# Second-layer input products by a seven-product block scheme for two of three token groups

## The chip, the core and the metric

The kernel runs on one core of a Trainium2 chip. The metric is the device time of one execution in microseconds (us), lower is better. The engines are named as in the profile: PE (TensorE, matrix products; PEld is its loading of weights), DVE (VectorE), ACT (ScalarE), POOL (GpSimd) and SP (the queue that issues DMAs). PE writes to PSUM, which has eight banks of 128 x 512 float32; DVE and ACT read them.

## What is computed

Attention with a local window and a few global keys over 2 batches, 8 heads and 768 tokens, and then two feed-forward layers on the 1536 x 512 result. The weights are float64 in memory, q, k and v float32.

```python
x = attn_out.transpose(0, 2, 1, 3).reshape(1536, 512)
h = x @ w_in                       # 512 x 2048
x = (h * (1 / (1 + exp(-h)))) @ w_out      # 2048 x 512
h = x @ w2_in
out = np.maximum(0.01 * h, h) @ w2_out
```

## The kernel before

**Numbers.** Every matrix is held as two float32r halves, a high part and a remainder (hi, lo), side by side in one tile `[128, 2, 512]`. A product takes three passes, hi x hi, lo x hi and hi x lo (`PASSES`, L103), so each 128-wide block of the inner dimension is three matmuls of 128 x 512. A remainder is one DVE subtraction after the copy that rounds the high part.

**Tiling.** The 1536 tokens are three groups (gi = 0, 1, 2) of 512. The 2048 inner columns are four parts of four chunks of 128. For each layer L, part and group, a *unit in* (`unit_in`, L286) multiplies the four 128-blocks of x with one chunk of w_in (12 matmuls into a bank `ph`), applies the nonlinearity (ACT L313 or L315, DVE L320 or L322) and splits the result into `g` (ACT L325, DVE L328). A *unit out* (`unit_out`, L339) multiplies the part's four `g` with w_out (12 matmuls into `po`) and adds to the running sum `y` (ACT L372 in the first part, DVE L390 after). After the last part of layer 0 the sum becomes the next x (`xn`, ACT L404, DVE L407); of layer 1 it is stored.

**Weights.** `load` (L240) brings one chunk of float64 into a stage tile `st` (SP), turns it into float32 `f` by bit operations (ACT L260, DVE L263, L266, L269), and splits it into `wi` or `wo` (the high part on ACT or DVE, L221 or L219; the remainder on DVE, L275). There are 3 stage buffers, 2 of `f`, 5 of `wi`, 6 of `wo`.

**Order.** `Sched.run` (L137) is a list scheduler that runs while the program is built: each task has an engine, a planned duration, a priority, dependencies and buffers (`SIZES`, L450, says how many); the order that it finds is written out, and every engine then works through its list in that order. The priorities of PE tasks rise with `pos` in the order in which `build` (L419) calls the units: two units of the next group, the four output units of this one, the other two units of the next group.

**Memory.** Attention's tiles (`ld`, `kT`, `a`, `sm`) lie in pools that stay open to the end; the running sums of group 2 reuse the `kT` tiles.

Of the kernel before, what the change touches and what calls it, by code (L numbers as in the profile page):

```python
# [16 lines left out]
P = 128  # L17
# [9 lines left out]
def kernel(  # L27
# [197 lines left out]
    class Moe:  # L225


        def __init__(self, sc, pools, xt, xdone, ykey):
            self.sc = sc
            self.wp, self.sp, self.cv, self.gp, self.tp, self.yp, self.xp, self.ps = pools  # L230
            self.ykey = ykey
# [5 lines left out]
            self.w, self.y, self.ydone, self.g = {}, {}, {}, {}  # L237
            self.pos = 100.0

        def load(self, which, L, fc, prio):  # L240
# [4 lines left out]
            f = Buf("f", lambda: self.cv.tile([P, DM], F32, tag="f", name="f"))  # L245
            w = Buf(tag, lambda: self.wp.tile([P, 2, DM], F32R, tag=tag, name=tag, bufs={"wi": 5, "wo": 6}[tag]))
# [37 lines left out]
            self.w[which, L, fc] = (w, t)  # L284

        def unit_in(self, n, j, c0=0, w=TG):  # L286
# [9 lines left out]
            if (n, j) not in self.g:  # L296
                self.g[n, j] = (Buf("g", lambda: self.gp.tile([P, 2, TG], F32R, tag="g", name="g")), [])
            g, gt = self.g[n, j]
# [40 lines left out]
        def unit_out(self, n, e, c0=0, w=TG):  # L339
# [26 lines left out]
            if part == 0:  # L366
                key = self.ykey(L, gi, e)
                y = self.y[gi, e] = Buf(key, lambda: self.yp.tile([P, TG], F32, tag=key, name="yp"))
# [7 lines left out]
                self.ydone[gi, e] = add("ACT", 0.55, evac, -1.0, (m,), (po, y))  # L376
                return
            y = self.y[gi, e]
            if not last:
# [14 lines left out]
            a = add("DVE", 0.07 + 0.55 * r, acc, -1.0, (m, self.ydone[gi, e]), (po, y, dst))  # L394
            self.ydone[gi, e] = a
            if not last:
                return
# [21 lines left out]
        def build(self, look, halves, first):  # L419

            for L in range(2):
                for part in range(NPART):
                    for which in ("in", "out"):
                        for j in range(FPP):
                            self.load(which, L, part * FPP + j, first(L, part, which, j))
            N = len(self.groups)

            def I(n, js):
                if n in halves:
                    for c0 in (0, 256):  # L430
                        for j in js:
                            self.unit_in(n, j, c0, 256)
                else:
                    for j in js:
                        self.unit_in(n, j)

            I(0, range(FPP))
            for n in range(N):
                if n + 1 < N:
                    I(n + 1, range(look))  # L440
                    for e in range(4):
                        self.unit_out(n, e)
                    I(n + 1, range(look, FPP))
                else:
                    for e in range(3):
                        self.unit_out(n, e)
                    self.unit_out(n, 3, 0, 256)
                    self.unit_out(n, 3, 256, 256)

    SIZES = {"st": 3, "f": 2, "wi": 5, "wo": 6, "g": 6, "t": 3, "ps": 8, "ld": 2, "qT": 3, "A": 2, "AT": 4, "sm": 4}  # L450
    for gi in range(NGR):
        for e in range(4):
            SIZES[f"x{gi}{e}"] = SIZES[f"y{gi}{e}"] = SIZES[f"k{e}"] = 1


    with ExitStack() as es:
# [7 lines left out]
        ld = pool("ld", 2)  # L464
        kp = pool("kT", 1)
        ap_ = pool("a", 2)
        sm = pool("sm", 4)
        ps = pool("ps", 8, space=PSUM)


        mask = const.tile([P, 256], F32, name="mask")
        mask0 = const.tile([P, P], F32, name="mask0")
# [43 lines left out]
        zero = const.tile([P, TG], mybir.dt.bfloat16, name="zero")  # L516
# [140 lines left out]
        def st_A(u):  # L657
# [45 lines left out]
            xdone[t0 // 2][hp].append((o, o + 256, add("DVE", 0.36, lo, n + 1.5, (h,), (pv, x))))  # L703
# [12 lines left out]
        def first(L, part, which, j):  # L716
            if L == 0 and part == 0:
# [3 lines left out]
        mo = Moe(sc, (wp, sp, cv, gp, tp, kp, xp, ps), xt, xdone,  # L721
                 lambda L, gi, e: f"k{e}" if gi == NGR - 1 else f"y{gi}{e}")
# [6 lines left out]
    with tc.If(general != 0), ExitStack() as es:  # L729
# [97 lines left out]
        for g in range(NGR):  # L827
            for hp in range(NHP):
                xb[g][hp].tile = xt[g][hp]
        mo = Moe(sc, (pool("gw"), pool("gstage", 3), pool("gcv", 2), pool("gg", 6), pool("gt", 3), pool("gyp"), xp, ps),  # L830
                 xb, done, lambda L, gi, e: f"y{gi}{e}")
# [33 lines left out]
```

## Time and profile before

| | |
|---|---|
| median of 3 runs (lowest to highest) | 630.77 us (630.51 to 631.47) |
| the profiled execution | 630.69 us |
| its span in the trace | 628.9 us |
| PE, DVE, ACT busy | 616.7, 432.8, 275.8 us |
| PE instructions (matmuls) | 3191 in the trace |

The span is what the trace covers, and 1.8 us of the execution lie outside it. A record of a matmul ends by a model and overlaps the next, so that the time that one costs is the distance between two starts. A few per cent of PE's records are missing from the trace, so a count in a row can be low. Everything up to about 140 us has attention and the first layer's first part interleaved; from there on PE does only units.

### The profile page before, as it was taken

To read this page: it belongs to the slowest core of one execution; us is meant where nothing else is said; L and a number is where in the kernel's file an instruction comes from. 1 tells how busy PE (TensorE), PEld (TensorE's weight loads), DVE (VectorE), ACT (ScalarE), POOL (GpSimd) and SP (SyncE) were. 2 spreads that over 40 slices of the span, in tenths; PEclk is the share of its full clock that TensorE was granted. 3 is DMA by queue.
4 is the path that set the end of the run, shared out by engine and by line. 5 is a ranking of instruction groups with operands and counts; after the bars stand their busy time and mean duration, and the time that the engine had idled before them with its cause. 6 is when DMAs were issued, how large, how long until landed. Compare 5 with 4: busy or idle time off the path is not lost.

```text
span 628.9 us, 8667 instructions
## 1 busy us (share of the span) xinstructions
PE 616.7 (98%) x3191; PEld 501.1 (80%) x3191; DVE 432.8 (69%) x993; ACT 275.8 (44%) x612; POOL 2.2 (0%) x18
## 2 busy tenths in 40 slices
PE   7999999999999999999999999999999999999996
PEld 4687777778888888888888888888888888888885
DVE  6999889889653967396748881776369745954333
ACT  5898878855541244124434453444233233213210
POOL 1000000000000000000000000000000000000000
PEclk8999999999999999999999999999999999999999
DMA  8976445213230323023302330133004110200112
GB/s 189 234 181 165 114 97 141 58 40 128 68 100 1 101 69 100 1 77 91 101 1 65 103 90 11 55 113 95 6 16 132 57 64 1 68 0 18 50 68 72
DMA packets 72673, 49.40 MB, mean 79 GB/s; under 512 B 50480, under 2 KB 67120, under 8 KB 72624
## 3 DMA queue, kind: packets, MB, share of 16 engines
q1 hardware_dynamic: 72336, 48.77, 28.0%
q8 instruction: 27, 0.44, 0.3%
q14 instruction: 22, 0.18, 0.1%
q10 hardware_dynamic: 288, 0.00, 0.0%
HBM read 45.62 MB, written 3.15 MB: 78 GB/s over the span
## 4 chain that ended last, share of the span: by engine, by line
PE 92%; DVE 6%; DMA 1%; issue 0%; ACTq 0%; DVEq 0%; ACT 0%
PE po L358 42%; PE ph L305 41%; PE s L618 3%; PE pa L670 3%; PE pv L690 3%; DVE A L630 1%; PE pt L576 1%; DVE A L653 1%; DVE f L266 1%; DMA nraw<-in_n_local_dram 1%; DVE f L269 0%; DVE wi L275 0%; DVE x L699 0%; DVE f L263 0%; DVE rs L644 0%
## 5 line engine op out<-in xcount | busy, mean ns | idle before, releaser
L305 PE MATMUL ph<-x,wi 128*128 128x512 f32 (+1 forms) x624 | 146.0, 379 | 1.2 <-DVE x L699 0.4
L358 PE MATMUL po<-g,wo 128*128 128x512 f32 x576 | 139.8, 392 | 0.0
L305 PE MATMUL ph<-xn,wi 128*128 128x512 f32 x576 | 136.9, 389 | 0.0
L358 PE MATMUL po<-wo,g 128*128 128x512 f32 (+1 forms) x588 | 136.4, 385 | 0.0
L305 PEld LDWEIGHTS ph<-x,wi 128*128 128x128 f32 x624 | 110.7, 188 | 24.7 <-issue 2.2
L358 PEld LDWEIGHTS po<-wo,g 128*128 128x128 f32 x588 | 108.9, 188 | 22.0
L305 PEld LDWEIGHTS ph<-xn,wi 128*128 128x128 f32 x576 | 108.1, 188 | 22.4
L358 PEld LDWEIGHTS po<-g,wo 128*128 128x128 f32 x576 | 107.1, 188 | 23.1 <-issue 1.3
L328 DVE TENSOR_TENSOR g<-t,g 128x512 fp32r<-128x512 f32 (+1 forms) x100 | 66.6, 669 | 41.5 <-ACT g L325 40.1
L325 ACT ACTIVATE g<-t 128x512 fp32r<-128x512 f32 (+1 forms) x100 | 61.2, 616 | 66.2 <-DVE t L322 37.8
L315 ACT ACTIVATE t<-ph 128x512 f32<-128x512 f32 x48 | 28.6, 596 | 91.4 <-PE ph L305 90.5
L322 DVE TENSOR_TENSOR t<-t,ph 128x512 f32<-128x512 f32 x48 | 32.9, 686 | 37.6 <-ACT t L315 37.6
L260 ACT ACTIVATE st<-st 128x512 f32<-128x512 f32 x64 | 43.0, 672 | 31.9 <-DMA st<-in_moe_w_out_dram 23.7
L390 DVE SCALAR_TENSOR_TENSOR yp<-po,yp 128x512 f32<-128x512 f32 x48 | 33.1, 689 | 32.2 <-PE po L358 32.2
L313 ACT ACTIVATE t<-ph 128x512 f32<-128x512 f32 (+1 forms) x52 | 29.2, 563 | 53.9 <-PE ph L305 53.2
L637 ACT ACTIVATE A<-A,nm 128x256 f32<-128x256 f32 (+1 forms) x96 | 46.3, 486 | 6.0 <-DVE nm L630 5.6
L266 DVE SCALAR_TENSOR_TENSOR f<-st,f 128x512 int32<-128x512 int32 x64 | 44.0, 690 | 1.2
L269 DVE SCALAR_TENSOR_TENSOR f<-st,f 128x512 int32<-128x512 int32 x64 | 43.9, 687 | 0.5
L320 DVE SCALAR_TENSOR_TENSOR t<-t,ph 128x512 f32<-128x512 f32 (+1 forms) x52 | 33.1, 644 | 15.1 <-ACT t L313 15.0
L630 DVE CUSTOM_DVE_ANT_0 A<-s,mask 128x256 f32<-128x256 f32 (+1 forms) x96 | 35.2, 396 | 6.8 <-PE s L618 6.7
L670 PE MATMUL pa<-ident,A 128*128 128x128 f32 x176 | 26.4, 279 | 3.6 <-DVE A L653 2.4
L390 DVE SCALAR_TENSOR_TENSOR yo<-po,yp 128x512 f32<-128x512 f32 (+1 forms) x25 | 16.7, 669 | 18.9 <-PE po L358 18.9
(67 smaller groups left out, 431.4 us busy)
## 6 DMA issues: line engine op xcount, KB each, us to landing
st<-in_moe_w_in_dram SPq DMA_DIRECT2D x32, 512.0 KB, 3.7
st<-in_moe_w_out_dram SPq DMA_DIRECT2D x32, 512.0 KB, 3.5
vd<-in_v_dram SPq DMA_DIRECT2D x24, 128.0 KB, 3.0
q<-in_q_dram SPq DMA_DIRECT2D x22, 128.0 KB, 3.0
k<-in_k_dram SPq DMA_DIRECT2D x22, 128.0 KB, 3.0
out_dram<-yo SPq DMA_DIRECT2D x11, 256.0 KB, 2.0
vp<-in_v_dram SPq DMA_DIRECT2D x20, 96.0 KB, 2.7
vp<-in_v_dram SPq DMA_DIRECT2D x20, 32.0 KB, 2.4
```

Of the source, the lines that this page charges most:

```text
L260: eng.activation(hf, hf, AF.Copy, scale=2.0 ** -112)
L266: eng.scalar_tensor_tensor(fi(), lo(), 29, fi(), op0=ALU.logical_shift_right, op1=ALU.bitwise_or)
L269: eng.scalar_tensor_tensor(fi(), hi(), -(2 ** 31), fi(), op0=ALU.bitwise_and, op1=ALU.bitwise_or)
L305: eng.matmul(ph()[:, :w], wv[:, a, kk, :], xs[kk]()[:, b, cs], start=(kk == 0 and i == 0), stop=(kk == NKK - 1 and i == 2),)
L320: eng.scalar_tensor_tensor(tt, tt, 1.0, ph()[:, :w], op0=ALU.add, op1=ALU.mult)
L325: eng.activation(g()[:, 0, cs], t()[:, :w], AF.Copy)
L328: eng.tensor_tensor(g()[:, 1, cs], t()[:, :w], g()[:, 0, cs].bitcast(F32), op=ALU.subtract)
L358: eng.matmul(po()[:, :w], lhsT, rhs, start=(j == 0 and i == 0), stop=(j == FPP - 1 and i == 2))
L390: eng.scalar_tensor_tensor(dst()[:, cs], po()[:, :w], scale, y()[:, cs], op0=ALU.mult, op1=ALU.add)
L630: eng.tensor_tensor_reduce(A()[:, i, j, c0:256], s[j]()[:, i, c0:256], mask0 if c0 else mask, -QSCALE * SLOPE[2 * hp + j], 3.0e38, ALU.add ...
L637: eng.activation(a, a, AF.Exp, bias=nm()[:, x:x + 1], scale=-1.0, accum_out=su()[:, x:x + 1])
L670: eng.transpose(pa()[:, j, c, :], A()[:, i, j, c * P:(c + 1) * P], ident)
```

## The change

The second layer's input products for groups 0 and 1 are done as 2 x 2 blocks. The rows of the block matrices are pairs of chunks of w_in, the inner dimension is split into two halves of 256 and the columns are the two groups. Strassen's scheme in Winograd's form needs seven products of 2 x 2 blocks in place of eight, on sums of weight blocks (S1 to S4) and sums of x blocks (T1 to T4). One such step is a *quad* (`unit_quad`): two chunks of weights, two groups, four results of 128 x 512.

- `combine`: after every second chunk of the second layer's w_in, DVE forms S1 to S4 (four operations on 128 x 256) and splits them into two tiles `ws`. 
- `sums`: at the end of the first layer DVE forms T1 to T4 from the running sums of groups 0 and 1, and they are split into `xs` tiles. T4 takes the place of one x block, which is no longer made by itself.
- `unit_quad`: seven products in four PSUM banks a to d. Banks a, c and d are used twice: p2, p3 and p4 add onto them once ACT (a) or DVE (c, d) has read the first product. ACT copies p1 out (L414), and DVE adds the rest in five operations (L415 to L417, L421, L422) in temporaries `tq`.
- `nonlin`: where a result lies in `tq`, the second layer's nonlinearity is one DVE operation (L449) and needs no ACT copy.
- Order in the second layer, per part: two quads, output units of group 0, four input units of group 2, output units of groups 1 and 2. The look-ahead of two units is not used there.
- Buffers: 4 `wi` and 5 `wo`. The pools of attention are closed when attention has ended, and a pool `late` opened in their place holds S, T, `tq`, two `gl` tiles and group 2's running sums. These wait for the last attention unit.

The core of the diff (`nonlin`, the pools and the branch for general masks are left out):

```diff
+        def combine(self, L, pair, prio):
...
+            for x in range(2):
+                sf = Buf("sf", lambda: self.late().tile([P, DM], F32, tag="sf", name="sf", bufs=SIZES["sf"]))
+                ws = Buf("ws", lambda: self.late().tile([P, 2, DM], F32R, tag="ws", name="ws", bufs=SIZES["ws"]))
+                if x == 0:
+                    s1 = sf
+                    ops = [(sf, 0, fb, 0, fb, 1, ALU.add), (sf, 1, sf, 0, fa, 0, ALU.subtract)]
+                else:
+                    ops = [(sf, 0, fa, 0, fb, 0, ALU.subtract), (sf, 1, fa, 1, s1, 1, ALU.subtract)]
...
+                h = add(AD, (0.52, 0.36), hi, prio, (t, *self.attn), (sf, ws))
+                res.append((ws, add("DVE", 0.62, lo, prio, (h,), (sf, ws))))
...
+        def sums(self, L):
...
+                    t = add("DVE", 0.62, sub, -0.5, (pt_, qt_), (f, pb, qb))
+                    h = add("ACT", 0.52, hi, -0.5, (t,), (f, x))
+                    self.T[i][kk] = (x, add("DVE", 0.62, lo, -0.5, (h,), (f, x)))
...
+                make(1, b[0, 1], b[0, 0])
+                make(2, b[1, 1], tmp[1])
+                make(4, b[1, 0], tmp[2])
+                make(3, b[1, 1], b[0, 1])
...
+        def unit_quad(self, n0, n1, L, pair):
...
+            p1 = prod("a", A11, X(0, 0), True)
+            p6 = prod("b", S2, T[2], True)
+            p5 = prod("c", S1, T[1], True)
+            p7 = prod("d", S3, T[3], True)
...
+            e1 = add("ACT", 0.55, lambda eng: eng.activation(u2(), ba(), AF.Copy), -1.0, (p1, *self.attn), (ba, u2))
+            tu2 = dve(lambda eng: eng.tensor_tensor(u2(), u2(), bb(), op=ALU.add), (e1, p6), (u2, bb))
+            tu4 = dve(lambda eng: eng.tensor_tensor(u4(), u2(), bc(), op=ALU.add), (tu2, p5), (u2, u4, bc))
+            c22 = dve(lambda eng: eng.tensor_tensor(u4(), u4(), bd(), op=ALU.add), (tu4, p7), (u4, bd))
+            p2 = prod("a", A12, X(0, 1), False, (e1,))
+            p3 = prod("c", S4, X(1, 1), False, (tu4,))
+            p4 = prod("d", A22, T[4], False, (c22,))
+            t12_ = dve(lambda eng: eng.tensor_tensor(c12(), u2(), bc(), op=ALU.add), (tu2, p3), (u2, c12, bc))
+            t21_ = dve(lambda eng: eng.tensor_tensor(u2(), u2(), bd(), op=ALU.add), (t12_, p4), (u2, bd))
+            for (nn, j, src, dep) in ((n0, j0, ba, p2), (n1, j0 + 1, u4, c22), (n1, j0, c12, t12_), (n0, j0 + 1, u2, t21_)):
+                self.nonlin(nn, j, src, dep, src is ba, L)
...
+            self.sums(1)
+            for part in range(NPART):
+                n = n1 + part * NGR
+                for x in range(FPP // 2):
+                    self.unit_quad(n, n + 1, 1, part * (FPP // 2) + x)
+                out(n)
+                I(n + 2, range(FPP))
+                out(n + 1)
+                out(n + 2)
+
+    SIZES = {"st": 3, "f": 2, "wi": 4, "wo": 5, "g": 6, "t": 3, "ps": 8, "qT": 3, "A": 2, "AT": 4, "tl": 4, "gl": 2,
+             "sf": 2, "ws": 2}
```

**What stands where.** The first place is PE in the second layer's second part. Before: the end of group 0's input units (the last slot of its fourth unit `ph_4357` is the first row), units of group 1 and the first output units of group 0 (`po_4425`, `po_4441`), with the third chunk's `g_4393` in the last row.

```order
L305 MATMUL ph_4357<-xn_3506,wi_4208 128x512 x3
L305 MATMUL ph_4384<-xn_3637,wi_3858 128x512 x3
L305 MATMUL ph_4401<-xn_3620,wi_4071 128x512 x3
L305 MATMUL ph_4384<-xn_3663,wi_3858 128x512 x3
L305 MATMUL ph_4401<-xn_3637,wi_4071 128x512 x3
L305 MATMUL ph_4384<-xn_3680,wi_3858 128x512 x3
L305 MATMUL ph_4401<-xn_3663,wi_4071 128x512 x3
L358 MATMUL po_4425<-wo_4139,g_4266 128x512 x3
L305 MATMUL ph_4401<-xn_3680,wi_4071 128x512 x3
L358 MATMUL po_4425<-wo_4167,g_4282 128x512 x3
L358 MATMUL po_4441<-wo_4139,g_4266 128x512 x3
L358 MATMUL po_4425<-wo_4316,g_4393 128x512 x3
```

After: the end of the part's second quad. Its bank d is `pq_4508` (p7, then p4), its bank c `pq_4475` (p3), and the output units of group 0 (`po_4496`, `po_4503` and so on) come in between.

```order
L390 MATMUL pq_4508<-xs_3759,ws_4455 128x512 x3
L390 MATMUL pq_4475<-xn_3680,ws_4455 128x512 x3
L531 MATMUL po_4496<-wo_4337,g_4480 128x512 x3
L390 MATMUL pq_4508<-xs_3691,wi_4254 128x512 x3
L531 MATMUL po_4496<-wo_4347,g_4512 128x512 x3
L390 MATMUL pq_4508<-xs_3748,wi_4254 128x512 x3
L531 MATMUL po_4503<-wo_4337,g_4480 128x512 x3
L531 MATMUL po_4551<-wo_4300,g_4447 128x512 x3
L531 MATMUL po_4503<-wo_4347,g_4512 128x512 x3
L531 MATMUL po_4551<-wo_4337,g_4480 128x512 x3
L531 MATMUL po_4565<-wo_4300,g_4447 128x512 x3
L531 MATMUL po_4496<-wo_4372,g_4559 128x512 x3
```

Between the last slot that a group's fourth `g` depends on and the first slot that reads it there were 12 slots of three matmuls (the reader of `g_4410`, the fourth, is two rows below the rows shown); now there are five, from the second row of p4 to the row with `g_4559`.

The second place is DVE at the same points. Before: the nonlinearity (L322) and the remainder (L328) of the units.

```order
L322 TENSOR_TENSOR t_4380<-t_4380,ph_4336 128x512
L328 TENSOR_TENSOR g_4393<-t_4380,g_4393 128x512
L322 TENSOR_TENSOR t_4399<-t_4399,ph_4357 128x512
L328 TENSOR_TENSOR g_4410<-t_4399,g_4410 128x512
L322 TENSOR_TENSOR t_4422<-t_4422,ph_4384 128x512
```

After: c22 (L417), C12 (L421), C21 (L422), the nonlinearities (L449) and the remainders (L455) of the second quad, and the first output sums.

```order
L417 TENSOR_TENSOR tq_4494<-tq_4494,pq_4508 128x512
L421 TENSOR_TENSOR tq_4528<-tq_4470,pq_4475 128x512
L449 SCALAR_TENSOR_TENSOR tq_4494<-tq_4494 128x512
L449 SCALAR_TENSOR_TENSOR tq_4528<-tq_4528 128x512
L455 TENSOR_TENSOR g_4538<-tq_4494,g_4538 128x512
L455 TENSOR_TENSOR g_4544<-tq_4528,g_4544 128x512
L422 TENSOR_TENSOR tq_4470<-tq_4470,pq_4508 128x512
L449 SCALAR_TENSOR_TENSOR tq_4470<-tq_4470 128x512
L455 TENSOR_TENSOR g_4559<-tq_4470,g_4559 128x512
```

Two DVE operations per chunk have become a row of nine for three results, and the `g` that PE wants first is the last of them.

The third place is ACT in the first quad of that part. Before: copies of units (L315, L325) with steps of weights (L260, L219) and output sums (L372) between.

```order
L260 ACTIVATE st_4251<-st_4251 128x512
L372 ACTIVATE yp_4295<-po_4258 128x512
L372 ACTIVATE yp_4307<-po_4274 128x512
L219 ACTIVATE wo_4327<-f_4221 128x512
L372 ACTIVATE yp_4333<-po_4297 128x512
```

After: the copy of p1 (L414), a first conversion step (L263) of a staged weight, the high part of the next weight sum (L219), and the scaled copy of bank a (L437).

```order
L414 ACTIVATE tq_4382<-pq_4357 128x512
L263 ACTIVATE st_4335<-st_4335 128x512
L219 ACTIVATE ws_4407<-sf_4263 128x512
L263 ACTIVATE st_4374<-st_4374 128x512
L437 ACTIVATE t_4428<-pq_4357 128x512
L452 ACTIVATE g_4440<-tq_4413 128x512
L263 ACTIVATE st_4400<-st_4400 128x512
L452 ACTIVATE g_4447<-t_4428 128x512
L219 ACTIVATE ws_4455<-sf_4274 128x512
```

Steps that wait for a DMA (L263) now stand ahead of copies that a quad's later products and results need.

## Rows read from the trace of the kernel before

**Rows 1.** The page: span, and busy time of each engine (share, instructions).
```profile
span 628.9 us, 8667 instructions
PE 616.7 (98%) x3191; PEld 501.1 (80%) x3191; DVE 432.8 (69%) x993; ACT 275.8 (44%) x612; POOL 2.2 (0%) x18
```

**Rows 2.** Busy time in four windows, second-layer parts (window, length, engines, PEclk, DMA).
```profile
357.19:422.47 65.28, 65.28 (x290) 54.07 (x288) 41.33 (x69) 29.48 (x49) 0.00 (x0) 1.00 0.23 71
422.47:487.75 65.28, 65.28 (x290) 54.07 (x288) 42.13 (x70) 22.87 (x39) 0.00 (x0) 1.00 0.22 65
487.75:553.03 65.28, 65.28 (x290) 54.07 (x288) 44.41 (x74) 19.21 (x33) 0.00 (x0) 1.00 0.14 44
553.03:618.31 65.28, 65.28 (x290) 54.07 (x288) 26.83 (x40) 13.79 (x23) 0.00 (x0) 1.00 0.09 33
```

**Rows 3.** The timeline of PE in the second layer (start, length, line, shapes, count).
```profile
368.07 9.68 PE L305 MATMUL ph<-xn,wi 128*128 128x512 f32 x42
...
389.83 9.68 PE L305 MATMUL ph<-xn,wi 128*128 128x512 f32 x42
```

**Rows 4.** The waits of PE (who waited for whom: total, times, longest).
```profile
PE pa L670 <- DVE A L653: 2.4, 1, 2.4
...
PE ph L305 <- DVE wi L275: 0.4, 1, 0.4
```

**Rows 5.** The timeline of DVE in three dense stretches.
```profile
76.39 0.42 DVE L699 TENSOR_TENSOR x<-pv,x 128x256 fp32r<-128x256 f32 x1
76.73 0.42 DVE L630 CUSTOM_DVE_ANT_0 A<-s,mask 128x256 f32<-128x256 f32 x1
...
271.29 0.68 DVE L328 TENSOR_TENSOR g<-t,g 128x512 fp32r<-128x512 f32 x1
271.90 0.68 DVE L320 SCALAR_TENSOR_TENSOR t<-t,ph 128x512 f32<-128x512 f32 x1
272.50 0.68 DVE L275 TENSOR_TENSOR wi<-f,wi 128x512 fp32r<-128x512 f32 x1
...
282.61 0.43 DVE L263 TENSOR_SCALAR f<-st 128x512 int32<-128x512 int32 x1
283.07 0.69 DVE L266 SCALAR_TENSOR_TENSOR f<-st,f 128x512 int32<-128x512 int32 x1
283.80 0.69 DVE L269 SCALAR_TENSOR_TENSOR f<-st,f 128x512 int32<-128x512 int32 x1
284.63 0.43 DVE L221 CAST wi<-f 128x512 fp32r<-128x512 f32 x1
285.09 0.69 DVE L275 TENSOR_TENSOR wi<-f,wi 128x512 fp32r<-128x512 f32 x1
285.70 0.68 DVE L320 SCALAR_TENSOR_TENSOR t<-t,ph 128x512 f32<-128x512 f32 x1
```

**Rows 6.** The timeline of all engines where one waits for another.
```profile
290.70 0.69 DVE L320 SCALAR_TENSOR_TENSOR t<-t,ph 128x512 f32<-128x512 f32 x1 [0.66 <-ACT t L313]
...
291.42 0.64 ACT L325 ACTIVATE g<-t 128x512 fp32r<-128x512 f32 x1 [0.75 <-DVE t L320]
...
292.09 0.69 DVE L328 TENSOR_TENSOR g<-t,g 128x512 fp32r<-128x512 f32 x1 [0.70 <-ACT g L325]
...
611.09 0.60 ACT L315 ACTIVATE t<-ph 128x512 f32<-128x512 f32 x1 [12.29 <-PE ph L305]
...
611.51 0.39 PE L358 MATMUL po<-wo,g 128*128 128x512 f32 x1
```

**Rows 7.** ACT's waits for staged weights, and landing times of those DMAs.
```profile
ACT st L260 <- DMA st<-in_moe_w_out_dram: 23.7, 9, 4.3
...
DMA to landing us min/median/max: 3.4/3.7/5.5
```

**Rows 8.** Busy time in windows of the start (columns as in rows 2).
```profile
10.00:12.00 2.00, 0.22 (x2) 0.17 (x2) 1.93 (x13) 2.00 (x8) 0.00 (x0) 1.00 1.31 216
12.00:14.00 2.00, 2.00 (x13) 2.00 (x13) 1.87 (x6) 1.62 (x7) 0.00 (x0) 0.62 1.00 229
14.00:16.00 2.00, 2.00 (x15) 1.44 (x15) 1.97 (x7) 1.36 (x4) 0.00 (x0) 0.53 1.09 355
16.00:18.00 2.00, 2.00 (x21) 1.49 (x17) 2.00 (x9) 1.48 (x4) 0.00 (x0) 1.00 1.33 237
```

More of the change, by code (lines that the diff above doesn't have):

```diff
@@ L284, in load, with fn, hi, lo @@
             self.w[which, L, fc] = (w, t)
+            self.f[fc % 2] = (f, t)
+            if which == "in" and L in self.quads and fc % 2:
+                self.combine(L, fc // 2, prio)
+        def combine(self, L, pair, prio):
+            add = self.sc.add
+            (fa, _), (fb, t) = self.f[0], self.f[1]
+            res = []
+            H = DM // 2
+            for x in range(2):
[6 more added lines that the diff above has]
+                    ops = [(sf, 0, fa, 0, fb, 0, ALU.subtract), (sf, 1, fa, 1, s1, 1, ALU.subtract)]
+                for (o, oh, p, ph, q_, qh, op) in ops:
+                    def fn(eng, o=o, oh=oh, p=p, ph=ph, q_=q_, qh=qh, op=op):
+                        half = lambda b, h: b()[:, h * H:(h + 1) * H]
+                        eng.tensor_tensor(half(o, oh), half(p, ph), half(q_, qh), op=op)
+                    t = add("DVE", 0.36, fn, prio, (t, *self.attn), tuple({id(b): b for b in (o, p, q_)}.values()))
+                def hi(eng, sf=sf, ws=ws):
+                    copy(eng, ws()[:, 0], sf())
+                def lo(eng, sf=sf, ws=ws):
+                    eng.tensor_tensor(ws()[:, 1], sf(), ws()[:, 0].bitcast(F32), op=ALU.subtract)
+                h = add(AD, (0.52, 0.36), hi, prio, (t, *self.attn), (sf, ws))
+                res.append((ws, add("DVE", 0.62, lo, prio, (h,), (sf, ws))))
+            self.w["sum", L, pair] = res
@@ new lines, in ypool, with gbuf @@
+        def ypool(self, gi):
+            return self.late() if self.late and gi == NGR - 1 else self.yp
+        def gbuf(self, n, j):
+            if (n, j) not in self.g:
+                if self.groups[n][0] in self.quads and j == FPP - 1:
+                    b = Buf("gl", lambda: self.late().tile([P, 2, TG], F32R, tag="gl", name="g", bufs=SIZES["gl"]))
+                else:
+                    b = Buf("g", lambda: self.gp.tile([P, 2, TG], F32R, tag="g", name="g"))
+                self.g[n, j] = (b, [])
+            return self.g[n, j]
@@ L374, in evac @@
                         eng.tensor_scalar(y(), po(), scale, None, op0=ALU.mult)
-                self.ydone[gi, e] = add("ACT", 0.55, evac, -1.0, (m,), (po, y))
+                self.ydone[gi, e] = add("ACT", 0.55, evac, -1.0, (m, *(self.attn if gi == NGR - 1 else ())), (po, y))
                 return
             y = self.y[gi, e]
-            if not last:
+            if not last or (L == 0 and 1 in self.quads and gi < 2):
                 dst = y
@@ L392, in acc @@
                 )
-            a = add("DVE", 0.07 + 0.55 * r, acc, -1.0, (m, self.ydone[gi, e]), (po, y, dst))
+            a = add("DVE", 0.07 + 0.55 * r, acc, -1.0, (m, self.ydone[gi, e]), (po, y, dst) if dst is not y else (po, y))
             self.ydone[gi, e] = a
-            if not last:
+            if not last or (L == 0 and 1 in self.quads and gi == 1 and e < 2):
                 return
@@ L453 @@
             SIZES[f"x{gi}{e}"] = SIZES[f"y{gi}{e}"] = SIZES[f"k{e}"] = 1
+    for i in range(1, 4):
+        for kk in range(2):
+            SIZES[f"T{i}{kk}"] = 1
     with ExitStack() as es:
@@ L719, in first @@
             return 30.0 + 8 * (L * NPART + part) + (4 if which == "out" else 0) + j
-        mo = Moe(sc, (wp, sp, cv, gp, tp, kp, xp, ps), xt, xdone,
-                 lambda L, gi, e: f"k{e}" if gi == NGR - 1 else f"y{gi}{e}")
+        mo = Moe(sc, (wp, sp, cv, gp, tp, yp, xp, ps), xt, xdone, late)
+        mo.attn = tuple(u["end"] for u in units)
         mo.build(2, (0,), first)
```

151 lines of the change are left out of this document (123 added, 28 removed).

## The prediction

> **What bounds the kernel now.** Read the busy shares first [rows 1]: PE 98%, DVE 69%, ACT 44%. A busy PE proves little, since its records overlap, so read its starts next [rows 3]. In the second layer 96 matmuls separate the two starts 368.07 and 389.83: 21.76 us, or 0.2267 us each, and three of them (one "slot" below: one block of the inner dimension, three passes) take 0.68 us. A part (three groups, in and out, 288 matmuls) therefore needs 65.28 us, and the four windows of that length tile the layer with one pattern and PE busy throughout [rows 2]. Third, the waits of PE: a few in the attention stage, the longest 2.4 us [rows 4], and none in the second layer. So all of the second layer is paced by the number of matmuls, and DVE has room: 41 to 44 us of 65 in the first three parts, 27 in the last [rows 2].
>
> The Trainium skill (TensorE: Matmul & The Clock Gate, Back-to-back issue gap) gives about 131 ns per 512-column matmul in a sustained stream, which would make the saving below 48 x 0.131 = 6.3 us and the time 625.8. The trace does not agree: 226.7 ns over the whole layer [rows 3], so this gets no chance among the rivals.
>
> **What is removed.** Per pair of weights, groups 0 and 1 took 4 units of 4 blocks x 3 passes = 48 matmuls; seven products of two blocks x 3 take 42. Eight pairs: 48 matmuls fewer, 48 x 0.2267 = **10.88 us**, all on the path. A part falls to 276 matmuls, 62.57 us.
>
> **What is added.** DVE gets five additions per quad (40), four half-width weight sums and two remainders per pair (32 and 16), and 16 operations on sums of x. Start to start an independent full DVE operation costs 0.60 us and a half one 0.34, although their busy times are 0.69 and 0.42; one that needs the DVE operation just before it costs 0.73, a CAST followed by its remainder 0.46 [rows 5]. Two remainders of x (1.2 us) and ten CASTs, which ACT takes over, fall away: 24.0 + 10.9 + 9.6 + 9.6 - 1.2 - about 4 = some 49 us more, mostly in the second layer. Counted in the order, a part's DVE rows come to about 58, 50, 50 and 29 us at these prices, against 62.57 us of PE. DVE fits on average, so its throughput is hidden behind PE. What is no longer hidden is latency, because two quads follow each other and the output units need their results at once.
>
> **The quad pair, walked.** I took the two quads of part 1 with time zero at the first product's first slot, PE at 0.68 us a slot, and these hops: end of a PE slot to the start of its reader 0.26 us (the unit's last slot ends one slot before 611.51, at 610.83, and ACT starts at 611.09 [rows 6]); DVE, then ACT, then DVE, 1.39 us from start to start [rows 6].
> - First quad: p7 ends at 6.80, so c22 starts at 7.06 and ends at 7.75. Its bank is needed by p4 at 8.16, after p2 and the first half of p3: 0.4 us spare.
> - Second quad: its p7 (planned at 17.0) needs the second pair of weight sums, whose buffer comes free at 9.5 when the first quad's p3 ends. Its remainder stands behind the first quad's DVE work and ends at 16.5: 0.5 us spare.
> - c22 of the second quad: p7 ends at 19.04, done 19.99; p4 wants the bank at 20.40: 0.4 us spare.
> - The tail: p4 ends at 22.44; before t21 DVE has two remainders of g that end their starts at 23.23; then t21, the second-layer nonlinearity, ACT's copy and the remainder: 23.23 + 0.73 + 1.39 + 0.69 = 26.04. PE wants this g after five more slots of output units, at 25.84: **0.2 to 0.3 us short**. Before, the same distance was 12 slots, 8.2 us, for a chain of 0.26 + 0.63 + 1.39 + 0.69 = 3.0 us.
>
> Parts 1 and 2 have this order, so 0.3 us each. In part 3, without weights to convert, the same walk gives 24.54 against 24.48: 0.1. In part 0 units of group 2 stand between (six slots before the late p7), which covers everything. At the layers' border the 16 DVE and 8 ACT operations on sums of x share the queues with group 2's last units: walked from the last output of group 1, the remainder of g for its third unit is ready at -6.6 and PE wants it at -6.8: 0.2 us. An exposed wait may add a restart. No row shows one alone in this stretch; the nearest is PE's 0.4 us wait for a weight [rows 4], so I take 0.1 for each of four places, from 0 to 0.4. Together 0.9 + 0.4 = **1.3 us**.
>
> **What moves at no cost, and its cover.** (a) One weight buffer fewer of each kind (5 to 4, 6 to 5). The first-layer order of PE after attention is the same. The tight one is w_out: after a part's last output unit, three weights rather than two must be finished before the next part's output, which starts 16 slots later and wants its fourth weight 3 slots after that, 12.9 us. A conversion done alone holds DVE from 282.61 to 285.70, 3.1 us [rows 5]; three plus eight DVE operations of units are 9.3 + 4.8 = 14.1, short by 1.2; with two of them converted up to their last two steps, as two f buffers allow, it is about 10, with slack. I take 0; the upper end is 1.2 at three borders, 3.6 us. (b) The y tiles of group 2 and all sums wait for the end of attention. Before, these y lay in the kT tiles and waited for attention too, and the order differs there by a few slots with the same count: 0. (c) On ACT 24 scaled copies of the units go; eight copies of p1, eight of the sums of x and 26 of weights and their sums come, two of x go: 16 more by the order's count, 0.6 us each [rows 6], on an engine that is 44% busy: 0. (d) DMA moves the same bytes and SP issues the same list; a landing takes 3.4 to 5.5 us [rows 7]. In the pair of quads a stage buffer comes free 5 to 6 us before ACT's step on it would hold up anything urgent, against a median of 3.7.
>
> **Sum.** 630.69 (the profiled execution; its span 628.9 and 1.8 around it) - 10.88 + 1.3 = 621.1; the median of the runs is 0.08 higher, so **621.2**.
>
> **Rivals.**
> 1. *The chain costs more than its hops.* If DVE must be counted at its busy 0.69 us per operation, the walk misses twice per pair: the second quad's p7 waits 0.7 us for its weight sum, the tail another 0.7. Four parts x 1.4 = 5.6 us: 630.8 - 10.9 + 5.6 = 625.5. For it: every spare above is under half a microsecond, and in a fixed order each delay is passed on. Against it: [rows 5] show 0.60 between starts wherever operations do not need each other. Buffer shortage (3.6 us alone, 623.5) lands in the same region.
> 2. *DVE becomes the bound.* Its fullest part, the first, has 58 us of DVE at 0.60 an operation; at the busy 0.69 that is 57.6 x 0.69 / 0.60 = 66.2 us, 3.7 more than PE needs, and with rival 1's 1.4 in each of the other three parts 7.9 in all: 627.8. With the buffers' 3.6 on top it is 631.4, no gain. Against it, again the start-to-start times [rows 5].
> 3. *Slower: ACT's queue held by a staged weight.* Between the copy of p1 and the weight-sum copy stands ACT's first conversion step, which waits for a DMA. ACT has waited for such a landing nine times, up to 4.3 us [rows 7], then with nothing urgent behind it; now the scaled copy of C11 and the weight sums are. A PE wait of that size also costs clock: after the 2.4 us wait the granted clock is 0.62 and 0.53 of full in the next two windows of 2 us, mostly the 1.2 GHz level, which is 1.7 us lost [rows 8]. So 4.3 + 1.7 = 6.0 us in each of the three parts with loads, 18 us: 637.9. It decides from 3.6 us per part. Against it: buffers come free early enough, see (d), and the bytes are unchanged.
>
> That the matmuls are not removed is excluded by the order: 2364 products of ph, po and pq before, 2316 now.
>
> **Numbers.** Forecast 621.2 (its own range 619.8 to 623), chance 0.71; rival 1, 625.5, 0.20; rival 2, 0.04, of which 0.03 with the buffers on top; rival 3, 637.9, 0.05. The range runs from 619.7 (no stall at all is 619.9) to 626.0, and leaves out most of rivals 2 and 3. About 0.2%, 1.3 us, is what a measurement tells from no change. Faster 0.92, within 0.2% 0.03, slower 0.05.
>
> **What would show it.** After: part windows of 62.6 us plus at most 0.5; PE waits on g, pq or ws that sum to 1 to 2 us, at the end of quad pairs and at the layers' border; DVE near 480 us busy; granted clock 1.00 in the second layer. Waits of 0.7 us on ws speak for rival 1; PE waits released by wo or wi in the first layer for the buffers; ACT idle on DMA in front of a quad and a clock under 1.00 for rival 3. I am wrong if the layer's parts are longer than 64 us, or if the first layer and attention end at another time than before.

## The result and the profile after

The changed kernel takes 620.75 us (median of 4 runs, 620.40 to 621.10), the kernel before 631.12 (630.51 to 631.76, with a fourth run beside the three of the table): a ratio of 0.9836, 95% interval 0.9818 to 0.9853. The forecast was 621.2. The profiled execution took 620.65, with a span of 618.7.

The page of the changed kernel (span, then busy time, share and instructions of each engine) answers to [rows 1]:

```profile
span 618.7 us, 8681 instructions
PE 606.2 (98%) x3143; PEld 492.2 (80%) x3143; DVE 474.3 (77%) x1085; ACT 283.0 (46%) x628; POOL 2.2 (0%) x18
```

PE has 48 matmuls fewer (3191 to 3143), DVE is 41.5 us busier, ACT has the 16 operations more that the order had shown. Four windows, one for each part of the second layer, answer to [rows 2], with the same columns:

```profile
361.00:423.56 62.56, 62.56 (x278) 51.79 (x277) 60.10 (x110) 31.82 (x54) 0.00 (x0) 1.00 0.33 103
423.56:486.12 62.56, 62.56 (x278) 51.80 (x277) 52.77 (x93) 22.36 (x38) 0.00 (x0) 1.00 0.21 66
486.12:548.68 62.56, 62.56 (x278) 51.80 (x277) 53.22 (x94) 22.24 (x38) 0.00 (x0) 1.00 0.18 60
548.68:611.24 62.56, 62.56 (x284) 52.04 (x282) 34.91 (x55) 13.29 (x23) 0.00 (x0) 1.00 0.11 41
```

PE is busy throughout each window, at a granted clock of 1.00. In the first part DVE is busy for 60.10 of 62.56 us, and still PE does not wait. I chose the windows' length, so how long a part takes is read from a second view, which does not rely on PE's overlapping records either: the run of 15 weight-sum matmuls that stands near the head of each part, and the last run of output matmuls, in PE's timeline of the changed kernel.

```profile
363.62 3.56 PE L390 MATMUL pq<-xs,ws 128*128 128x512 f32 x15
...
426.20 3.56 PE L390 MATMUL pq<-xs,ws 128*128 128x512 f32 x15
...
488.76 3.56 PE L390 MATMUL pq<-xs,ws 128*128 128x512 f32 x15
...
551.33 3.56 PE L390 MATMUL pq<-xs,ws 128*128 128x512 f32 x15
...
592.80 20.03 PE L531 MATMUL po<-wo,g 128*128 128x512 f32 x99
```

The distances are 62.58, 62.56, 62.57 and 41.47 us, and 62.57 is 276 x 0.2267: a part takes 62.57 us where it took 65.28, and **no part holds a stall**. These four distances are the ruler for the experiments; below, "lost in part n" is the same distance in another kernel minus this one.

Between the two profiled executions lie 630.69 - 620.65 = 10.04 us, 0.84 less than 48 matmuls. PE's work does not explain the rest. Take the output slot near the end of the first layer that stands in the same place in both kernels, and the end of the last run of output matmuls (the kernel before, then the changed one, whose last run is shown above):

```profile
345.63 0.84 PE L358 MATMUL po<-g,wo 128*128 128x512 f32 x3
...
612.87 10.52 PE L358 MATMUL po<-wo,g 128*128 128x512 f32 x57
```

```profile
345.94 0.84 PE L531 MATMUL po<-g,wo 128*128 128x512 f32 x3
```

From one to the other are 612.87 + 10.52 - 345.63 = 277.76 us before and 592.80 + 20.03 - 345.94 = 266.89 after: 10.87 less, so the layers' border holds no stall either. The 0.84 lies outside: the slot comes 0.31 later in this execution, which is within what executions differ by (see the end of this document), and 0.5 more lies behind PE's last run, for which no cause is shown.

### The profile page after: what moved, and what is told of

Its sections match the earlier page's. It is cut to its first block, busy times and chain, and to the rows that moved or that the text cites. A ratio compares the mean times of both kernels' runs of the same rounds, so it can differ in the third digit from the quotient of the medians.

```text
span 618.7 us, 8681 instructions
## 1 busy us (share of the span) xinstructions
PE 606.2 (98%) x3143; PEld 492.2 (80%) x3143; DVE 474.3 (77%) x1085; ACT 283.0 (46%) x628; POOL 2.2 (0%) x18
## 4 chain that ended last, share of the span: by engine, by line
PE 92%; DVE 5%; DMA 1%; issue 0%; SPq 0%; ACTq 0%; DVEq 0%; ACT 0%
PE po L531 42%; PE ph L478 28%; PE pq L390 12%; PE s L821 3%; PE pa L873 3%; PE pv L893 3%; PE pt L779 1%; DVE A L833 1%; DVE A L856 1%; DVE f L269 1%; DMA nraw<-in_n_local_dram 1%; DMA k<-in_k_dram 0%; DVE f L272 0%; DVE wi L278 0%; DVE f L266 0%
## 5 line engine op out<-in xcount | busy, mean ns | idle before, releaser
L563 DVE SCALAR_TENSOR_TENSOR yp<-po,yp 128x512 f32<-128x512 f32 x56 | 38.5, 688 | 27.4 <-PE po L531 27.4
L498 ACT ACTIVATE g<-t 128x512 fp32r<-128x512 f32 (+1 forms) x68 | 40.8, 606 | 40.6 <-DVE t L493 29.6
L501 DVE TENSOR_TENSOR g<-t,g 128x512 fp32r<-128x512 f32 (+1 forms) x68 | 44.3, 657 | 14.2 <-ACT g L498 13.6
L263 ACT ACTIVATE st<-st 128x512 f32<-128x512 f32 x64 | 42.7, 668 | 22.7 <-DMA st<-in_moe_w_out_dram 21.7
L478 PE MATMUL ph<-xn,wi 128*128 128x512 f32 x192 | 46.6, 389 | 0.0
L478 PEld LDWEIGHTS ph<-xn,wi 128*128 128x128 f32 x192 | 36.0, 188 | 7.5
L390 PE MATMUL pq<-xs,ws 128*128 128x512 f32 x144 | 36.7, 389 | 0.0
L219 ACT ACTIVATE wo<-f 128x512 fp32r<-128x512 f32 x25 | 15.7, 632 | 40.0 <-PE po L531 18.4
L390 PEld LDWEIGHTS pq<-xs,ws 128*128 128x128 f32 x144 | 27.0, 188 | 5.6
```

The source lines that it names most:

```text
L263: eng.activation(hf, hf, AF.Copy, scale=2.0 ** -112)
L390: eng.matmul(bank[c]()[:, :], wv[:, a, 2 * half + kk, :], Bx[kk][0]()[:, b, :], start=(first and kk == 0 and i == 0), stop=(kk == 1 and i ...
L478: eng.matmul(ph()[:, :w], wv[:, a, kk, :], xs[kk]()[:, b, cs], start=(kk == 0 and i == 0), stop=(kk == NKK - 1 and i == 2),)
L498: eng.activation(g()[:, 0, cs], t()[:, :w], AF.Copy)
L501: eng.tensor_tensor(g()[:, 1, cs], t()[:, :w], g()[:, 0, cs].bitcast(F32), op=ALU.subtract)
L563: eng.scalar_tensor_tensor(dst()[:, cs], po()[:, :w], scale, y()[:, cs], op0=ALU.mult, op1=ALU.add)
```

## The experiments

The forecast was right in size, but 1.3 us of it were stalls that are not there: the waits of PE that it named as its sign do not occur. So the questions were two. Is the gain only the 48 matmuls, or do buffers and order carry a part? And how near are the stalls: was the walk through the quad pair wrong by a little or by much? Where an experiment repeats an operation, it computes the same value again. The code shown is cut to the lines that matter; a condition that the program hands down as an argument stands in its place.

**Buffers alone.** The changed kernel's pools, with eight products and the old order:

```
- self.quad = late is not None
+ self.quad = False
```

> The changed kernel's buffers (4 w_in and 5 w_out tiles, attention's pools closed early, group 2's partial sums in the late pool), but all sixteen of the kernel before's eight-product block products and its order of the second layer. My theory (the gain is the 48 matmuls and nothing else; buffers cost nothing): within 0.6 us of the kernel before, 630.5 to 631.7, no TensorE wait outside attention. Rival (fewer weight buffers cost, and the changed kernel's other savings pay for it): 632 to 634.7, with TensorE waits for weight remainders in the layers.

Measured 631.32 (ratio to before 1.0002, interval 0.9992 to 1.0012), and PE waits for nothing behind 125 us. From the slot named above to the end of PE's last run it takes 277.76 us, as the kernel before does. Fewer weight buffers and pools in attention's place cost nothing that can be measured. The rival falls.

**Order alone.**

```
- self.sums(1)
...
- self.unit_quad(n, n + 1, 1, part * (FPP // 2) + x)
+ for j in (2 * x, 2 * x + 1):
+     self.unit_in(n, j)
+     self.unit_in(n + 1, j)
```

> The changed kernel's buffers and its order of the second layer (groups 0 and 1 side by side, no products of the next group ahead of the output products), but eight products in place of seven, without the sums and the additions. My theory: 288 matmuls a part again, so 48 x 0.2267 = 10.9 us over the changed kernel, 631.6, and 630.8 to 632.4 with the spread of runs. Rival A (part of the gain comes from the new order): 630 or less. Rival B (the new order costs something that the additions happen to hide): 632.8 or more, with TensorE waits at the border of the layers or at the ends of the input products.

Measured 631.61 (ratio 1.0005, interval 0.9995 to 1.0015), again without a PE wait behind 125 us. From this kernel to the changed one only the seven products and what they need (sums, additions, copies) differ: 631.61 - 620.75 = 10.86 us. The runs of this kernel spread from 630.39 to 632.12, so the medians alone are good to about half a microsecond. The distance on PE is sharper:

```profile
345.59 0.84 PE L531 MATMUL po<-g,wo 128*128 128x512 f32 x3
...
602.63 20.72 PE L531 MATMUL po<-wo,g 128*128 128x512 f32 x102
```

It is 602.63 + 20.72 - 345.59 = 277.76 us again, against 266.89: 10.87 us, or 0.2265 us for each of 48 matmuls, the 0.2267 of [rows 3]. The order carries none of the gain. The Trainium skill (TensorE: Matmul & The Clock Gate, Back-to-back issue gap) has about 131 ns for a sustained stream, which gives an estimate of 6.3 us here; the runs disagree with it.

**Is the tail near the path?** The forecast had PE wait 0.2 to 0.3 us for the last remainder of g. In the trace of the changed kernel that remainder comes as late as forecast (DVE, ACT and DVE of the last result of part 1, then PE's run of output matmuls that needs it):

```profile
448.00 0.69 DVE L449 SCALAR_TENSOR_TENSOR tq<-tq 128x512 f32<-128x512 f32 x1
...
448.73 0.63 ACT L452 ACTIVATE g<-tq 128x512 fp32r<-128x512 f32 x1 [2.08 <-DVE tq L449]
...
449.39 0.69 DVE L455 TENSOR_TENSOR g<-tq,g 128x512 fp32r<-128x512 f32 x1 [0.70 <-ACT g L452]
...
446.61 7.64 PE L531 MATMUL po<-wo,g 128*128 128x512 f32 x33
```

It is ready at 450.08. The slot that reads it is the sixth of the run at 446.61 and starts at 446.61 + 5 x 0.680 = 450.01, so PE should have waited. But a slot is three passes, high x high, low x high, high x low, and in the program's order only the third waits on DVE: 450.01 + 2 x 0.2267 = 450.46. To test this, the low part of g is read first:

```
- for i, (a, b) in enumerate(PASSES):
+ for i, (a, b) in enumerate(PASSES if L == 0 else ((0, 1), (0, 0), (1, 0))):
```

> The changed kernel with the passes of the second layer's output products in the order hi x lo, hi x hi, lo x hi, so that the remainder of g is read by the first matmul of a slot and not by the third, 0.45 us later; all else, DVE's and ScalarE's orders too, is the same. My theory (the forecast stall of 0.2 to 0.3 at the tails of parts 1 and 2 is absent only because the third pass reads the remainder: done at 450.08, slot at 450.01, third matmul at 450.46): TensorE waits 0.1 to 0.3 in parts 1 and 2 at the slot that follows the last addition of the second quad pair, none in part 0, 0 to 0.1 in part 3; together 0.2 to 0.6, so 621.0 to 621.4. Rival (the tail is not near the path at all, and the walk of it was wrong): no wait, 620.75.

Measured 621.31 in one execution, with a span of 619.5 (0.8 more than the changed kernel's). One execution proves little by its time, since those of the changed kernel spread over 0.7 us; the distances within its trace do more. Lost in the four parts: 0.01, 0.27, 0.25, 0.25. PE, DVE and the weight loads (PEld) of that kernel in part 1:

```profile
446.53 7.91 PE L531 MATMUL po<-wo,g 128*128 128x512 f32 x33
...
455.64 9.68 PE L478 MATMUL ph<-xn,wi 128*128 128x512 f32 x42
...
449.32 0.69 DVE L455 TENSOR_TENSOR g<-tq,g 128x512 fp32r<-128x512 f32 x1 [0.70 <-ACT g L452]
...
450.06 3.95 PEld L531 LDWEIGHTS po<-wo,g 128*128 128x128 f32 x18 [0.40 <-DVE g L455]
```

The stall appears, of the size forecast, and in part 3 too, where I had expected 0 to 0.1. PE's own rows show no wait for it: g is the weight operand here, so the weight load waits, 0.40 us until 0.05 us after the remainder, and PE's record merely grows from 7.64 to 7.91. **The stall was hidden by the order of the passes alone.** With 0.05 for the hop and the 0.19 that a load lasts, I estimate that a remainder is wanted 0.24 us ahead of its matmul, so the changed kernel would have 450.46 - 450.08 - 0.24 = 0.14 us to spare, not the 0.38 that I first read.

**The spare at the tail, by a larger dose.** The last remainder of each part's second quad three times:

```
+ for _ in range(3 if pair % 2 and nn == n0 and j == j0 + 1 else 1):
      eng.tensor_tensor(g()[:, 1, :], t(), g()[:, 0, :].bitcast(F32), op=ALU.subtract)
```

> The changed kernel with the remainder of the last result of each part's second quad pair computed three times in place of once: 2 x 0.60 us more on the chain addition, leaky ReLU, high part, remainder, and nothing else changed in order or result. My theory (the spare there is 450.46 - 450.08 = 0.38 in parts 1 and 2, about 0.9 in part 3, over 1.2 in part 0): TensorE waits of 0.8 to 1.0 in parts 1 and 2, 0.3 to 0.5 in part 3, none in part 0, together 2.1 (1.6 to 2.6): 622.8. With the forecast's own spare (0.2 to 0.3 short in parts 1 and 2, and 0.1 in part 3): 1.4 to 1.5 in each of two parts and 1.3 in the third, over 4 in all: 625. Rival (the chain is off the path): no wait, 620.75.

Measured 625.60 (ratio 0.9910, interval 0.9894 to 0.9927), 4.85 over the changed kernel. Lost in the parts: 1.29, 1.30, 1.29, 1.24. My expectation of 2.1 fell; it had counted neither the load ahead of the matmul nor the repeated operation at 0.73 each, and it had nothing in part 0. DVE in part 1 (line numbers from here on can be one higher than in the changed kernel), and all waits of the weight loads from 340 us on:

```profile
450.65 2.15 DVE L456 TENSOR_TENSOR g<-tq,g 128x512 fp32r<-128x512 f32 x3 [0.70 <-ACT g L452]
...
393.77 2.37 PEld L532 LDWEIGHTS po<-wo,g 128*128 128x128 f32 x11 [0.94 <-DVE wo L278]
397.64 5.08 PEld L532 LDWEIGHTS po<-wo,g 128*128 128x128 f32 x23 [0.54 <-DVE wo L278]
452.85 3.54 PEld L532 LDWEIGHTS po<-wo,g 128*128 128x128 f32 x16 [1.39 <-DVE g L456]
516.73 3.52 PEld L532 LDWEIGHTS po<-wo,g 128*128 128x128 f32 x16 [1.40 <-DVE g L456]
579.14 3.54 PEld L532 LDWEIGHTS po<-wo,g 128*128 128x128 f32 x16 [1.32 <-DVE g L456]
```

Three take 2.15 us, one 0.69: 1.46 more, of which 1.24 to 1.30 is lost. So the spare at the ends of parts 1 to 3 is 0.16 to 0.22 us, near the estimate of 0.14. In part 0, which the walk had called covered, the loss is as large and stands elsewhere: DVE is full there, and w_out's remainders come late.

**The spare at p7.** The remainder of the second weight sum of each second pair three times. (In the text on record "541.40" should read 441.40.)

```
+ for _ in range(3 if x == 1 and pair % 2 else 1):
      eng.tensor_tensor(ws()[:, 1], sf(), ws()[:, 0].bitcast(F32), op=ALU.subtract)
```

> The changed kernel with the remainder of the second weight sum (S3, S4) of each part's second quad pair computed three times in place of once; the order and the result are the same. It is the operation for which the forecast read 0.5 us of spare in front of the product p7. The remainders of the output products showed that the weight operand has to be there some 0.24 us ahead of the matmul that uses it (0.05 to the load, 0.19 for the load), and that three such operations take 1.46 us longer than one. My theory: second matmul of the slot minus the end of the remainder minus 0.24 leaves 541.40 - 440.86 style spares of 0.5 in part 1 and 2, none in part 0 (380.61 + 0.69 + 0.24 = 381.54, matmul at 381.54) and 1.9 in part 3; so 0.9 to 1.0 lost in parts 1 and 2 each, 1.2 to 1.5 in part 0, none in part 3, together 3.3 (2.6 to 3.8): 624.0. Rival (ahead of a product of the quad the wait is hidden by other work that TensorE has): 620.75 to 621.2. Rival (VectorE as a whole is the bound, so each added microsecond costs one wherever it is): 4 x 1.46 = 5.8, 626.6.

Measured 625.37 (ratio 0.9904, interval 0.9888 to 0.9921), 4.6 over the changed kernel and more than the 2.6 to 3.8 that I expected. Lost: 1.39, 0.91, 1.14, 1.18. Parts 0 and 1 are as expected, part 2 nearly: what is not lost of the 1.46, the spare at p7, is 0.07 in part 0, 0.55 in part 1, 0.32 in part 2, against the forecast's 0.5. In part 3, which makes most of the miss, I had expected nothing. There the sum itself is early, but the additions stand behind it on DVE, and p3 waits for the one of p5 (L417 here, L416 in the changed kernel), which has to read bank c before p3 may add onto it (PE's waits: total, times, longest):

```profile
PE pq L391 <- DVE ws L317: 2.5, 3, 1.1
...
PE pq L391 <- DVE tq L417: 0.9, 1, 0.9
```

**VectorE's sum, where I took it to be idle.** Every remainder of group 2's hidden tiles in parts 1 to 3 of the second layer, three times in place of once:

```
+ for _ in range(3 if L == 1 and part and self.quad else 1):
      eng.tensor_tensor(g()[:, 1, cs], t()[:, :w], g()[:, 0, cs].bitcast(F32), op=ALU.subtract)
```

> The changed kernel with the remainder of every hidden tile of group 2 in parts 1 to 3 of the second layer computed three times in place of once: 12 x 1.46 = 17.5 us more VectorE work, three times that of the other experiment, but in the stretch where TensorE works on group 2's input products and group 1's output products and VectorE is idle between two units. The order and the result are the same. My theory (what counts is the chain through the quad pairs, not VectorE's sum): 620.75, at most 621.3. Rival (VectorE's sum is the bound or close to it, 482 us of a span of 619): 630 or more if it is the bound throughout, 624 if half of it shows.

Measured 630.32 (ratio 0.9986, interval 0.9976 to 0.9995): 9.6 us, and my theory in this form fell. The time is the rival's (630 or more), but not for its reason: lost in the profiled execution are 0, 0, 4.92 and 4.97, so DVE does not bound throughout. Each loss stands at the head of the next part, and the dose in part 3, with no part behind it, shows in none. The timeline of PE and ACT at the head of part 2, and two windows of 2 us there:

```profile
489.22 3.56 PE L390 MATMUL pq<-xs,ws 128*128 128x512 f32 x15
495.88 1.65 PE L390 MATMUL pq<-xn,wi 128*128 128x512 f32 x3 [3.10 <-ACT tq L414]
497.33 1.48 PE L390 MATMUL pq<-xs,ws 128*128 128x512 f32 x3
498.61 1.02 PE L390 MATMUL pq<-xn,wi 128*128 128x512 f32 x3
...
494.71 0.63 ACT L219 ACTIVATE wo<-f 128x512 fp32r<-128x512 f32 x1 [1.34 <-DVE f L272]
495.25 0.58 ACT L414 ACTIVATE tq<-pq 128x512 f32<-128x512 f32 x1
```

```profile
496.00:498.00 2.00, 2.00 (x5) 1.61 (x6) 2.00 (x5) 0.90 (x2) 0.00 (x0) 0.50 0.83 252
498.00:500.00 2.00, 2.00 (x8) 1.50 (x7) 2.00 (x4) 1.02 (x2) 0.00 (x0) 0.76 0.17 34
```

Read from below: ACT's copy of p1 (L414), which p2 needs, stands in ACT's queue behind the copy of a staged w_out tile (L219), and that one waits for DVE. The copy ends 495.25 + 0.58 - 489.22 = 6.61 us after the weight-sum run begins, where it ended 1.32 after in the changed kernel, so 5.3 of the 5.84 us added to DVE arrive here. PE idles 3.1 us: p2 starts at 495.88 and not at 489.22 + 3.40 = 492.62, 3.26 late. Behind the wait the granted clock is 0.50, the 1.2 GHz level, and then 0.76, and the first two slots take 1.45 and 1.28 us in place of 0.68, 1.37 more. Together that is 4.63 of the 4.92 us lost. And the late staged weight has its cause in DVE, which was hardly idle where I had put the load. In the trace of the changed kernel DVE is busy for 27.36 of the 28 us from 464 to 492 and through the next 11, with the next part's weights:

```profile
464.00:492.00 28.00, 28.00 (x125) 23.17 (x125) 27.36 (x53) 10.48 (x18) 0.00 (x0) 1.00 0.36 113
492.00:503.00 11.00, 11.00 (x50) 9.13 (x49) 11.00 (x19) 6.75 (x12) 0.00 (x0) 1.00 0.31 97
503.00:515.00 12.00, 12.00 (x54) 9.93 (x54) 8.94 (x14) 2.66 (x5) 0.00 (x0) 1.00 0.00 0
```

Most of its idle time lies behind the quads, from 503 on. p1's last slot was over when the weight-sum run began at 489.22, yet its copy starts at 495.25, behind L219. The Trainium skill (TensorE: Matmul & The Clock Gate, Architectural detail) has ACT's queue as strictly first in, first out, and these rows agree.

**Half the dose,** to tell ACT's queue from DVE's chain (`range(2 ...)` in the same place):

> As the run with three remainders for each hidden tile of group 2 in parts 1 to 3, but with two: 4 x 0.73 = 2.9 us more VectorE work in each of the three parts, 8.8 in all; the order and the result are the same. What is open is why the larger dose cost 9.6 us. Theory A (VectorE is full from the end of group 2's inputs to the next part's quads, so that its delay arrives there whole, less 0.55 us of idle time; what then stops TensorE first is the copy of p1 on ScalarE, which stands in the queue behind a staged weight's copy and has 2.0 us to spare): at the borders to parts 2 and 3 the copy of p1 is 2.4 late, TensorE waits 0.3 to 0.4 for it, the clock keeps its level, and the rest of the delay, some 1.6, shows at the additions and weight sums of the quads, whose spares are 0 to 0.5; together 1.5 to 2 in each of the two parts, 624 to 625. Theory B (ScalarE's queue alone holds TensorE): 0.3 to 0.4 in each, 621.4. Theory C (a cost in proportion to VectorE's added work, 9.6 / 17.5): 4.8, 625.6, spread over parts 1 to 3.

Measured 623.09 (ratio 0.9873, interval 0.9856 to 0.9889), 2.3 over the changed kernel. Lost: 0.01, 0.00, 2.04, 0.77. All waits of the weight loads from 340 us on, and the first slots on PE behind the first of them:

```profile
492.10 0.53 PEld L390 LDWEIGHTS pq<-xn,wi 128*128 128x128 f32 x3 [0.62 <-ACT tq L414]
495.16 0.53 PEld L390 LDWEIGHTS pq<-xn,ws 128*128 128x128 f32 x3 [1.15 <-DVE tq L416]
496.36 0.53 PEld L390 LDWEIGHTS pq<-xs,wi 128*128 128x128 f32 x3 [0.67 <-DVE tq L417]
556.73 0.53 PEld L390 LDWEIGHTS pq<-xn,wi 128*128 128x128 f32 x3 [0.63 <-ACT tq L414]
559.70 0.53 PEld L390 LDWEIGHTS pq<-xs,wi 128*128 128x128 f32 x3 [0.38 <-DVE tq L417]
...
492.11 0.96 PE L390 MATMUL pq<-xn,wi 128*128 128x512 f32 x3 [0.20 <-ACT tq L414]
492.91 0.85 PE L390 MATMUL pq<-xs,ws 128*128 128x512 f32 x3
```

Theory A in mechanism: first ACT's copy (PE itself waits 0.2 us for it in each part, expected 0.3 to 0.4), then the additions. In size it holds for part 2 (1.5 to 2 expected) and not for part 3 (0.77), so the sum is under its 624; why part 3 lost less is not shown. Theory B gives 0.7 in all and is out; C, with 4.8 spread over three parts, is out too, since part 1 loses nothing.

**The same step in the first layer.** If each quad pair is worth its six matmuls as long as DVE's chain fits, groups 0 and 1 of the first layer should pay as well:

```
+ def isq(self, L, part):
+     return self.quad and (L == 1 or part >= self.q0)       # q0 = 2, or 1
...
+ def sub0(eng):                       # sums of x from its high and low parts
+     eng.tensor_tensor(f(), ph, qh, op=ALU.subtract)
+     eng.tensor_tensor(f(), f(), pl, op=ALU.add)
+     eng.tensor_tensor(f(), f(), ql, op=ALU.subtract)   # T1, T3; two operations for T2, T4
...
- self.sums(1)
- for part in range(NPART):
+ self.sums(0)
+ for n in range(n1, N, NGR):          # n1 = q0 * NGR
+     L, part, _ = self.groups[n]
+     if n == N // 2:
+         self.sums(1)
```

> The same seven products also for groups 0 and 1 in parts 2 and 3 of the first layer: 24 fewer matmuls more; the sums of x are built from the high parts and remainders of attention's output, 28 VectorE operations once. My theory (each quad pair takes 6 matmuls off TensorE's path as long as VectorE's chain fits): 24 x 0.2267 = 5.44 off 620.75 gives 615.3, and up to 617 if the denser VectorE of the first layer leaves spares of nothing at the parts' ends, as in part 0 of the second layer. Rival (the first layer's longer chain, with tanh on ScalarE, eats the gain): 619 or more.

Measured 615.65 (ratio 0.9754, interval 0.9738 to 0.9770), as expected; the rival falls.

> As the one before, for parts 1 to 3 of the first layer: 36 fewer matmuls than the changed kernel, with the sums of x in part 0's and 1's VectorE time, right behind attention. My theory: 36 x 0.2267 = 8.16 off 620.75 gives 612.6, and 612.3 to 615 with stalls where VectorE is dense behind attention. Rival (VectorE behind attention is already full, so part 1's quads cost more than their 2.72): over 615.3, that is, over the version with parts 2 and 3 alone.

Measured **613.53** (ratio 0.9721, interval 0.9705 to 0.9737), the fastest kernel of this study: 7.2 us under the changed kernel for 36 matmuls, 8.16 by count, and within the 612.3 to 615 expected. PE on its page, and the waits of its weight loads behind 125 us that the changed kernel does not have (who waited for whom: total, times, longest):

```profile
PE 598.9 (98%) x3107; PEld 484.8 (79%) x3107; DVE 522.1 (85%) x1176; ACT 299.3 (49%) x657; POOL 2.2 (0%) x18
```

```profile
PEld pq L411 <- DVE tq L437: 0.7, 2, 0.4
PEld pq L411 <- DVE tq L438: 0.5, 2, 0.3
PEld po L552 <- DVE g L522: 0.4, 1, 0.4
```

The small spares are used up: four loads of quads now wait for additions, and one, just ahead of the first quads, for the remainder of an ordinary unit (L522), 1.6 us in all. That is of the order of the 0.9 that is missing from 8.16, if these waits cost PE less than their length, as the 0.40 us above that cost 0.27; it was not measured wait by wait. DVE is at 85%; I expect that the next step of this kind would have to take work from DVE first.

## Why the prediction was right, point by point

- *48 matmuls at 0.2267, all on the path.* Right, and measured alone: 10.87 us on PE between eight and seven products in the same order.
- *DVE fits on average.* Right: 201.0 us busy in the four windows against 250.2 of PE. By part it was 60.1, 52.8, 53.2 and 34.9 busy where the count at issue had 58, 50, 50 and 29. Its 41.5 us more on the page is less than the 49 counted; why was not looked into.
- *The quad pair, walked.* The times of the walk hold: the remainder at the tail was forecast 26.04 us after the part's first product slot (424.17), and came at 25.91; the spare of 0.5 at p7 measured 0.55 and 0.32. **The term that was mis-sized is the stall, 1.3 us, which is 0.** The step that failed is "PE wants this g after five more slots": the slot begins then, but its remainder is read by the third matmul, 0.45 us later. With the remainder read first 0.77 us appears at the three tails for which the walk had 0.7. The border's 0.2 is not there: the 266.89 us across it are 48 matmuls short of 277.76 and nothing else. The same slip may explain it, since there too a slot reads the remainder in its third pass; this was not tested. The restarts fell away with the waits; where a wait was made, the 0.1 taken for one was near (0.80 us from 492.11 to 492.91 for a slot of 0.68).
- *Part 0 is covered.* Only just: DVE has next to nothing to spare there, and 1.46 us more on either place cost 1.29 and 1.39.
- *Buffers and pools at nothing.* Right (1.0002).
- *Rivals 1 and 2.* Not what happened, but their point of decision is near: 0.16 to 0.22 us at the tails. The reason against them, 0.60 us from start to start [rows 5], holds: DVE goes through part 0 almost without a gap, and PE does not wait.
- *Rival 3.* Not in the changed kernel. Its mechanism is real: with 5.8 us more of DVE work in a part ACT's queue held the copy of p1, PE waited 3.1 us, and with the lower clock behind it 4.9 were lost. I had it wait for a DMA and decide from 3.6 us; the staged weight waited for DVE, and the copy's spare in the changed kernel is 2.1 us (done at 489.50 + 0.58 = 490.08, p2's slot at 488.76 + 3.40 = 492.16):

```profile
489.50 0.58 ACT L414 ACTIVATE tq<-pq 128x512 f32<-128x512 f32 x1
```

- *The sign "if the first layer and attention end at another time".* By the letter it came: the first layer ends 0.31 us later. It is the level of that execution and not the change, as the last section shows.
- *The size, 0.45 us off, is in part luck.* Without the missing stall the forecast would have been 619.9, 0.9 too low. The three runs that it started from had a low median, 630.77; over the 19 runs of the kernel before that were taken with the first experiments it is 631.24, from which 48 matmuls leave 620.4, at the low end of the changed kernel's runs (620.40 to 621.10). The 1.3 us of stall that is not there made up for that.

## What to carry to other kernels

Here, where PE is paced by matmuls, a scheme with fewer products was worth its matmuls (10.87 us on PE for 10.88 by count) as long as the chain on the other engines ended ahead of PE. Where it did not quite, in the kernel with the first layer's parts too, 36 matmuls were worth 7.2 of 8.16 us. Count that spare at the matmul (and its weight load) that reads the operand, not at the unit's start, and read the operand that comes last in the last pass. An engine's share says little on its spare: at 77% DVE had 39 us with hardly a gap around the quad pairs' begin, and of 5.84 us added there 5.3 reached the next part's first copy on ACT, which had 2.1 to spare. When a change has spares of tenths of a microsecond, dose them on purpose before building on top of it.

## What the runs showed of the hardware

- A wait on a weight operand does not show as PE's wait when it is short: 0.40 us on PEld, 0.27 lost, no row among PE's waits. Distances between landmarks on PE showed it.
- The same DVE operation issued three times on one output takes 2.15 us, 0.73 from start to start, as an operation that needs the one before [rows 5], not the 0.60 of independent ones; my dose was 20% larger than meant.
- Attention and the first layer take a few tenths of a microsecond more or less from one execution to the next. The output slot near the first layer's end, in the runs with three and with two remainders for each hidden tile of group 2, which up to there have the changed kernel's order on PE, DVE and ACT:

```profile
346.40 0.84 PE L532 MATMUL po<-g,wo 128*128 128x512 f32 x3
```

```profile
345.52 0.84 PE L532 MATMUL po<-g,wo 128*128 128x512 f32 x3
```

The changed kernel has it at 345.94, the kernel before at 345.63, both within this spread of 0.88 us. What in an execution sets its level is not shown.
